# The second half block's softmax: one exponential per group of columns, its sum taken by ScalarE, its later steps moved back one slot

## The chip, the cores and the metric

The kernel runs on one core of a Trainium2 chip. The metric is the device time of one execution in microseconds (us); lower is better. The kernel before has a median of 837.12 us in three runs (836.88 to 837.44).

## The reference, cut to what matters

The reference is a linear attention with 32 memory slots, followed by a gated MLP and a mixture of eight experts. The part that this change touches is the second softmax, over the 32 memory slots of each token and head:

```python
scores = scale * np.matmul(q, k_m.transpose(0, 1, 3, 2))
scores = scores - np.max(scores, axis=-1, keepdims=True)
attn = np.exp(scores)
attn = attn / (np.sum(attn, axis=-1, keepdims=True) + 1e-09)
return np.matmul(attn, v_m).astype(np.float32)
```

Its result is the `x` of the gated MLP, `(silu(x @ w_gate) * (x @ w_val)) @ w_out`, whose hidden width of 1536 is worked off in 12 pieces of 128.

## The kernel before, in words

The 2304 tokens are cut into eight half blocks of 288 tokens (BT). Half block `i` goes through the gated MLP in 12 slots `f` (0 to 11), one for each piece of the hidden width. While half block `i` is in its slots, the softmax of half block `i+1` is prepared between them. The order of all work is written out by hand: the schedule is manual, each engine executes its instructions in the order in which the program issues them, and an engine whose next instruction waits holds back everything behind it.

`put(i, n, fn, ...)` (L688) files a step for half block `i` at time `n`; slot `f` covers the times from 2f to 2f+2. `run(i, n)` (L691) issues all steps filed up to `n`, in the order of their times. `slot0(f)` (L866) is the body of a slot of half block 0. It issues, in this order:

- the steps up to time 2f;
- in even slots the projection of the value memory (`proj_a`, L427: matmuls L346 into `pp`; `proj_h`, L435: two ScalarE copies L438; `proj_b`, L440: two VectorE subtractions L443);
- `down(0, f-2)` (L495): four matmuls L502 into `acc`;
- unpacking of arriving weights: `top(n)` (L198) is a ScalarE copy at L204, `low(n)` (L206) the VectorE instruction at L208 that needs it; in slot 9 `low(31)` and `low(32)` stand here, in slot 10 `top(33)` and `low(33)`;
- `gv(0, f)` (L469): six matmuls L473 into `pg` (PSUM bank 4), six into `pv` (bank 5), then ScalarE's Tanh of `pg` (L481);
- the steps up to 2f+1.5;
- `gate_act(0, f)` (L484): on VectorE L486, which reads `pg`, and L487, which reads `pv`;
- in slots 10 and 11 `step(34)` and `step(35)` (L857), each a `top` and its `low`;
- the steps up to 2f+1.99.

The first slot of half block 1, `slot1(1, 0)` (L895), issues `gv(1, 0)` at once. It writes the same banks 4 and 5, so its first matmul waits for the L486 of slot 11. It reads the finished softmax `X[1]`; in the order `ALL` (L466) the matmuls 1 to 3 into `pg` read group g=0 (high part, low part, high part), and 4 to 6 read g=1 (high, low, high).

The softmax of one group `g` (four heads) of one half block has these steps, on a tile `sm` of 128 partitions by 9 groups of 32 columns:

- `s2_a` (L366): VectorE's maximum over each 32 columns (L370) and its subtraction (L371);
- `s2_e` (L374): ScalarE's exponential, one instruction of 288 columns (L375);
- `s2_b` (L394): `s2_sum` (L377: VectorE's sum of each 32 columns at L379, L380 adds 1e-9, L381 takes the reciprocal) and `s2_norm` (L383: product L386 and 32x32 transpose L391, both VectorE);
- `s2_c` (L398): ScalarE's rounded copy, the high part of `X` (L401);
- `s2_d` (L403): VectorE's subtraction, the low part of `X` (L404).

A table `AT["s2"]` (L50) gives their times. Its row 0 is for half block 1, prepared in half block 0, and is read by this loop:

```python
        for g in range(2):
            for m, fn in zip((n[2], n[3], *n[4 + 3 * g:7 + 3 * g]), (s2_a, s2_e, s2_b, s2_c, s2_d)):
                if fn is s2_b and isinstance(m, tuple):
                    put(i - 1, m[0], s2_sum, i, g)
                    put(i - 1, m[1], s2_norm, i, g)
                else:
                    put(i - 1, m[g] if isinstance(m, tuple) else m, fn, i, g)
```

At 23.6 of half block 0, `s1_a` of the next batch entry is filed: two VectorE maxima of 576 columns (L270). Its exponentials `s1_e` (L275) already use ScalarE's running sum (`accum_out`), which gives an ACTIVATE and a separate ACTIVATION_READ_ACCUMULATOR.

Of the kernel before, what the change touches and what calls it, by code (L numbers as in the profile page):

```python
# [14 lines left out]
AF = mybir.ActivationFunctionType  # L15
OP = mybir.AluOpType
AX = mybir.AxisListType
# [3 lines left out]
B, H, S, D, M = 4, 8, 576, 64, 32  # L21
# [5 lines left out]
BT = S // 2  # L27
# [20 lines left out]
        2: (9, 9.92, 13.2, 13.9, 15, 17.9, 19, 19.9, 21, 21.9, 23, 23.9, 25, 25.9, 27),  # L48
    },
# [25 lines left out]
def moe_program(ctx, tc, xin, wa, wgn, nz, wb, out):  # L75
# [10 lines left out]
    V, A, P, G, Q = nc.vector, nc.scalar, nc.tensor, nc.gpsimd, nc.sync  # L86
# [251 lines left out]
    SM, X = {}, {}  # L338
# [33 lines left out]
        SM[i, g] = (sm, rd)  # L372

    def s2_e(i, g):  # L374
        A.activation(SM[i, g][0], SM[i, g][0], AF.Exp, scale=1.0 / D ** 0.5)  # L375

    def s2_sum(i, g):  # L377
        sm, rd = SM[i, g]
        V.tensor_reduce(rd[:, 1, :], sm, axis=AX.X, op=OP.add)  # L379
        V.tensor_scalar(rd[:, 1, :], rd[:, 1, :], 1e-9, None, op0=OP.add)  # L380
        V.reciprocal(rd[:, 2, :], rd[:, 1, :])  # L381

# [11 lines left out]
    def s2_b(i, g):  # L394
        s2_sum(i, g)
        s2_norm(i, g)
# [331 lines left out]
    for b in range(1, B):  # L728
        i = 2 * b - 2
# [11 lines left out]
        for j, o in enumerate(AT["proj"][b]):  # L741
            i, f = 2 * b - 1 + o // NF1, o % NF1
# [3 lines left out]
    for i in range(1, NB):  # L746
        if i > 1:
            put(i - 1, 6, load_q, i)
        n = AT["s2"].get(i - 1, AT["s2"][2])
        put(i - 1, n[0], s2_p, i)  # L750
        put(i - 1, n[1], s2_t, i)
# [33 lines left out]
    s1_cv(0, 1, 0, A)  # L785
    spin(6)
    s2_e(0, 0)
    s1_d(0, 1, 0)
    s1_dc(0, 1, 0)
# [11 lines left out]
    s1_cv(0, 1, 1, A)  # L801
    spin(14)
    s2_e(0, 1)
    s1_dc(0, 0, 1)
    s1_d(0, 1, 1)
# [748 lines left out]
```

## Time and profile before

| | |
|---|---|
| median of three runs | 837.12 us (836.88 to 837.44) |
| the profiled execution, its own time | 836.54 us |
| span of its trace | 834.7 us |
| PE busy | 820.9 us (98%) |
| DVE busy | 637.0 us (76%) |
| ACT busy | 391.8 us (47%) |
| slots 8 to 11 of half block 0 in the trace | 55.4 to 71.0 us |

PE is TensorE, DVE is VectorE, ACT is ScalarE. Times inside the trace count from the span's start. Matmuls are pipelined: each record is longer than the distance to the next one. Durations of ACT and DVE records overlap a little too, so a sum over a run of instructions is made from starts, not from durations.

### The profile page before, as it was taken

What the parts mean: (1) busy time and instruction counts of PE and PEld (TensorE: products, weight loads), DVE (VectorE), ACT (ScalarE), POOL (GpSimd) and SP (SyncE); (2) the same over time, 40 slices, a digit from 0 to 9 for tenths busy, and PEclk for the clock granted to TensorE, in tenths of its full rate; (3) what the DMA queues carried; (4) which work ended last, traced back from release to release, by engine and by line L of the source; (5) the groups of instructions that cost most, each with busy time, mean ns of one, the idle gap of its engine ahead of it and who ended that gap; (6) DMA issues with size and microseconds to landing.
All of it is one profiled execution on the core that took longest, in us unless ns stands there. A gap on an engine that the chain in (4) does not pass through costs nothing.

```text
span 834.7 us, 16643 instructions
## 1 busy us (share of the span) xinstructions
PE 820.9 (98%) x6317; PEld 730.7 (88%) x6317; DVE 637.0 (76%) x1534; ACT 391.8 (47%) x804; POOL 244.7 (29%) x345
## 2 busy tenths in 40 slices
PE   7999999999999999999999999999999999999996
PEld 5777988999899998999999988888888888888885
DVE  5887688776867677868684597898889988899761
ACT  5765565343443334333444555555455454554430
POOL 2000012424233252453122233123315233145132
PEclk9999999999999999999999999999999999999999
DMA  9993649775426373448747973555465644654421
GB/s 350 400 397 122 204 161 327 234 247 142 116 67 216 84 212 96 120 127 217 233 160 217 237 202 91 127 144 128 101 166 131 144 128 94 161 143 111 159 84 65
DMA packets 79145, 143.20 MB, mean 172 GB/s; under 512 B 16176, under 2 KB 36880, under 8 KB 79056
## 3 DMA queue, kind: packets, MB, share of 16 engines
q1 hardware_dynamic: 59696, 100.66, 38.4%
q0 software_dynamic: 19360, 41.38, 20.5%
q8 instruction: 52, 0.85, 0.4%
q14 instruction: 37, 0.30, 0.1%
HBM read 105.34 MB, written 36.68 MB: 170 GB/s over the span
## 4 chain that ended last, share of the span: by engine, by line
PE 89%; DMA 7%; DVE 2%; issue 1%; ACT 1%; SPq 0%; POOL 0%; POOLq 0%; DVEq 0%; ACTq 0%
PE acc L1190 18%; PE ph L1176 17%; PE acc L506 16%; PE pg L473 9%; PE pv L473 8%; PE acc L1005 7%; PE ph L987 7%; PE pp L346 2%; DMA out<-pv,ix 1%; DMA early<-wa 1%; DMA stw<-wa 1%; PE pT L528 1%; DMA stx<-wa 1%; DMA stg<-wa 1%; PE pkv L310 1%; DMA qt<-xin 1%
## 5 line engine op out<-in xcount | busy, mean ns | idle before, releaser
L1190 PE MATMUL acc<-ws,hs 128*128 128x512 f32 (+1 forms) x690 | 174.9, 394 | 0.0
L1176 PEld LDWEIGHTS ph<-xh,ws 128*128 128x128 f32 x1008 | 150.9, 188 | 9.7 <-ACT y L1213 0.7
L1176 PE MATMUL ph<-xh,ws 128*128 128x308 f32 x1008 | 157.4, 304 | 0.3 <-ACT y L1213 0.3
L1190 PEld LDWEIGHTS acc<-ws,hs 128*128 128x128 f32 (+1 forms) x690 | 122.7, 184 | 24.3
L506 PE MATMUL acc<-a,ro 128*128 128x288 f32 x576 | 116.4, 295 | 0.0
L1030 POOL DMA_INDIRECT out<-pv,ix x40 | 63.0, 1575 | 177.8 <-ACT pv L1022 67.5
L506 PE MATMUL acc<-a,os 128*128 128x288 f32 x432 | 106.0, 295 | 0.0
L473 PE MATMUL pg<-x,pt 128*128 128x288 f32 x576 | 101.3, 310 | 0.7 <-DVE a L486 0.2
L473 PEld LDWEIGHTS pg<-x,pt 128*128 128x128 f32 x576 | 81.0, 188 | 18.3 <-issue 6.4
L506 PEld LDWEIGHTS acc<-a,ro 128*128 128x128 f32 x576 | 92.1, 188 | 0.0
L473 PE MATMUL pv<-x,pt 128*128 128x288 f32 x576 | 91.9, 295 | 0.0
L473 PEld LDWEIGHTS pv<-x,pt 128*128 128x128 f32 x576 | 81.7, 188 | 0.0
L670 POOL DMA_INDIRECT xs<-R,gidx x48 | 48.1, 1003 | 111.5 <-DMA xs<-R,gidx 93.6
L486 DVE SCALAR_TENSOR_TENSOR ta<-ta,pg 128x288 f32<-128x288 f32 x84 | 37.6, 448 | 55.0 <-ACT ta L481 54.9
L506 PEld LDWEIGHTS acc<-a,os 128*128 128x128 f32 x432 | 74.1, 189 | 0.3 <-ACT ro L459 0.2
L481 ACT ACTIVATE ta<-pg 128x288 f32<-128x288 f32 x84 | 34.4, 410 | 82.2 <-PE pg L473 82.1
L492 ACT ACTIVATE a<-ta 128x288 fp32r<-128x288 f32 x84 | 37.3, 444 | 68.9 <-DVE ta L487 68.8
L463 POOL DMA_DIRECT2D os<-osl x72 | 40.8, 567 | 97.3 <-PE acc L506 56.0
L987 PE MATMUL ph<-xt,wm 128*128 128x384 f32 (+1 forms) x256 | 55.4, 307 | 0.0
L987 PEld LDWEIGHTS ph<-xt,wm 128*128 128x128 f32 x256 | 43.7, 189 | 2.6
L487 DVE TENSOR_TENSOR ta<-ta,pv 128x288 f32<-128x288 f32 x84 | 38.1, 454 | 8.8
L493 DVE TENSOR_TENSOR a<-ta,a 128x288 fp32r<-128x288 f32 x84 | 37.5, 447 | 5.8 <-ACT a L492 5.6
(241 smaller groups left out, 1448.1 us busy)
## 6 DMA issues: line engine op xcount, KB each, us to landing
wb<-wb SPq DMA_DIRECT2D x70, 512.0 KB, 4.4
os<-osl POOLq DMA_DIRECT2D x72, 256.0 KB, 3.4
kv<-xin SPq DMA_DIRECT2D x16, 576.0 KB, 6.5
xl<-xs SPq DMA_DIRECT2D x40, 160.0 KB, 6.7
stg<-wa SPq DMA_DIRECT2D x12, 511.8 KB, 10.2
out<-zt SPq DMA_DIRECT2D x1, 5888.0 KB, 24.7
xd<-R SPq DMA_DIRECT2D x8, 603.0 KB, 5.6
qt<-xin SPq DMA_DIRECT2D x8, 576.0 KB, 6.9
```

Source lines behind the costliest of these rows:

```text
L463: G.dma_start(r(lo), r(osl[f][:, :]))
L473: P.matmul(p, r(PT[f // 2, g][:, w, f % 2, 128 * a:128 * a + 128]), r(X[i][:, s, g, :]), start=(n == 0), stop=(n == 5))
L486: V.scalar_tensor_tensor(ta, ta, 1.0, pg, op0=OP.add, op1=OP.mult)
L487: V.tensor_mul(ta, ta, pv)
L493: V.tensor_sub(r(ah[:, 1, :]), ta, ah[:, 0, :])
L506: P.matmul(ACC[i][c], r(OS[i, f][w][:, o]), r(ah[:, s, :]), start=(f == 0 and n == 0), stop=(f == NF1 - 1 and n == 2))
L670: G.indirect_dma_start(out=xs[:, :], out_offset=bass.IndirectOffsetOnAxis(ap=RT[i][:, t, n:n + 1], axis=0), in_=R[i][:, t, :], in_offset=None)
L987: P.matmul(p, r(w[:, c]), r(x[:, k, b, :]), start=(m == 0), stop=(m == 11))
L1005: P.matmul(AC2[e, t][:h], r(a[:, o:o + h]), r(b), start=(f == 0 and m == 0), stop=(f == NF2 - 1 and m == 2))
L1030: G.indirect_dma_start(out=out, out_offset=bass.IndirectOffsetOnAxis(ap=IX[e][:h, t:t + 1], axis=0), in_=PV[e, t][:h], in_offset=None, com ...
L1176: P.matmul(out, r(w[i][:, c + 128 * k:c + 128 * k + 128]), r(x[:, m, k, a]), start=(start and n == 0), stop=(n == 5), skip_group_check=not ...
L1190: P.matmul(AC2[e, t][:h], r(a[:, n, o]), r(w[b][:, n]), start=(f == 0 and m == 0), stop=(f == NF2 - 1 and m == 2))
```

## The change

The times of the softmax steps of half block 1 become later. For group 0: the exponential from 17.1 (slot 8) to 19 (slot 9), `s2_b` from 19 to 21 (slot 10), `s2_c` from 19.9 to 21.02, `s2_d` from 21 to 21.9. For group 1: `s2_a` from 17.9 to 19.9, the exponential from 19 to 21.1, `s2_b` from 21.1 to 23 (slot 11), `s2_c` from 21.9 to 23.05, `s2_d` from 23 to 23.9. In this half block alone the exponential becomes nine instructions of 32 columns, each with ScalarE's running sum written into `rd`, and VectorE's sum (L379) goes. The other seven half blocks keep theirs.

```diff
     "s2": {
-        0: (13.9, 14, (17, 17.9), (17.1, 19), 19, 19.9, 21, 21.1, 21.9, 23),
+        0: (13.9, 14, (17, 19.9), (19, 21.1), 21, 21.02, 21.9, 23, 23.05, 23.9),
...
     def s2_e(i, g):
-        A.activation(SM[i, g][0], SM[i, g][0], AF.Exp, scale=1.0 / D ** 0.5)
+        sm, rd = SM[i, g]
+        if i == 1:
+            for a in range(BT // M):
+                A.activation(sm[:, a, :], sm[:, a, :], AF.Exp, scale=1.0 / D ** 0.5, accum_out=rd[:, 1, a:a + 1])
+        else:
+            A.activation(sm, sm, AF.Exp, scale=1.0 / D ** 0.5)
 
     def s2_sum(i, g):
         sm, rd = SM[i, g]
-        V.tensor_reduce(rd[:, 1, :], sm, axis=AX.X, op=OP.add)
+        if i != 1:
+            V.tensor_reduce(rd[:, 1, :], sm, axis=AX.X, op=OP.add)
         V.tensor_scalar(rd[:, 1, :], rd[:, 1, :], 1e-9, None, op0=OP.add)
         V.reciprocal(rd[:, 2, :], rd[:, 1, :])
```

## Rows read from the trace of the kernel before

**Rows 1.** The page: busy time of each engine.

```profile
PE 820.9 (98%) x6317; PEld 730.7 (88%) x6317; DVE 637.0 (76%) x1534; ACT 391.8 (47%) x804; POOL 244.7 (29%) x345
```

**Rows 2.** Busy time by stretch: start:end, length, PE, PEld, DVE, ACT, POOL, clock, DMA.

```profile
77.00:400.00 323.00, 322.97 (x3149) 296.91 (x3149) 235.29 (x751) 135.65 (x333) 104.10 (x214) 1.00 0.58 173
400.00:815.00 415.00, 414.75 (x2362) 369.90 (x2361) 339.20 (x652) 206.18 (x376) 129.40 (x105) 1.00 0.57 146
```

**Rows 3.** Timeline of VectorE, slots 9 to 11: start, duration, line, tiles.

```profile
60.43 1.28 DVE L208 SCALAR_TENSOR_TENSOR wa<-stg,top 128x512 int32<-128x512 int32 x2
...
62.11 0.17 DVE L380 TENSOR_SCALAR rd<-rd 128x9 f32<-128x9 f32 x1
...
63.46 0.42 DVE L486 SCALAR_TENSOR_TENSOR a<-a,pg 128x288 f32<-128x288 f32 x1
...
65.74 0.68 DVE L208 SCALAR_TENSOR_TENSOR ro<-stx,top 128x512 int32<-128x512 int32 x1
66.34 0.45 DVE L404 TENSOR_TENSOR x<-at,x 128x288 fp32r<-128x288 f32 x1
66.70 0.44 DVE L379 TENSOR_REDUCE rd<-sm 128x9 f32<-128x288 f32 x1
...
70.03 0.45 DVE L404 TENSOR_TENSOR x<-at,x 128x288 fp32r<-128x288 f32 x1
70.54 0.45 DVE L486 SCALAR_TENSOR_TENSOR a<-a,pg 128x288 f32<-128x288 f32 x1
...
71.47 0.69 DVE L208 SCALAR_TENSOR_TENSOR ro<-stx,top 128x512 int32<-128x512 int32 x1
72.07 1.41 DVE L270 TENSOR_REDUCE st<-phi 128x1 f32<-128x576 f32 x2
73.39 0.44 DVE L486 SCALAR_TENSOR_TENSOR ta<-ta,pg 128x288 f32<-128x288 f32 x1
```

**Rows 4.** Timeline of ScalarE, slots 9 to 11; in brackets the idle time before.

```profile
60.55 0.44 ACT L375 ACTIVATE sm<-sm 128x288 f32<-128x288 f32 x1
63.57 0.44 ACT L401 ACTIVATE x<-at 128x288 fp32r<-128x288 f32 x1 [2.58 <-DVE at L391]
63.92 1.07 ACT L438 ACTIVATE pt<-pp 128x512 fp32r<-128x512 f32 x2
...
70.40 0.77 ACT L204 ACTIVATE top<-stx 128x512 f16<-128x512 bf16 x1
```

**Rows 5.** The chain that ended last, in order of time, around slot 11's end.

```profile
71.05 1.06 PE pg L473 x6
72.11 0.80 PE pv L473 x6
72.91 1.94 PE acc L502 x8
```

**Rows 6.** Timeline of ScalarE: one exponential with running sum, and the next one's start.

```profile
72.85 0.78 ACT L275 ACTIVATE phi<-phi,st 128x576 f32<-128x576 f32 x1 [0.29 <-DVE st L270]
73.53 0.19 ACT L275 ACTIVATION_READ_ACCUMULATOR phi<-phi,st 128x1 f32 x1
73.63 0.76 ACT L275 ACTIVATE phi<-phi,st 128x576 f32<-128x576 f32 x1
```

**Rows 7.** Groups of ScalarE's instructions by form: busy us, mean ns of one, idle before.

```profile
L375 ACT ACTIVATE sm<-sm 128x288 f32<-128x288 f32 x16 | 6.6, 438 | 1.7 <-DVE sm L371 1.7
...
L568 ACT ACTIVATE gex<-ga 96x24 f32<-96x24 f32 x8 | 1.7, 208 | 0.0
```

**Rows 8.** Busy time by stretch again, where TensorE idles; PE second, clock eighth column.

```profile
15.00:16.00 1.00, 0.24 (x8) 0.08 (x8) 0.68 (x2) 0.97 (x2) 0.00 (x0) 1.00 1.02 414
...
827.00:828.00 1.00, 0.76 (x4) 0.26 (x2) 0.20 (x1) 0.00 (x0) 0.10 (x1) 1.00 0.35 131
...
830.00:831.00 1.00, 0.00 (x0) 0.00 (x0) 0.00 (x0) 0.00 (x0) 0.71 (x1) 1.00 0.00 0
831.00:832.00 1.00, 0.00 (x0) 0.00 (x0) 0.00 (x0) 0.00 (x0) 0.00 (x0) 0.53 0.64 148
```

## The prediction, as put on record before the changed kernel ran

> **What bounds the kernel now.** I read the page first, then busy time by stretch, the chain, and the timelines of VectorE and ScalarE around the change. The page has TensorE busy for 98% of the span [rows 1]. The stretches after the change's place say more: from 77 to 815 us TensorE is busy for 737.7 of 738 us [rows 2]. So whatever delays TensorE before 77 us is not made up later; it arrives at the end in full.
>
> The change lies in slots 9 to 11 of half block 0, about 60 to 71 us. There VectorE works with hardly a gap [rows 3] and ScalarE has one long idle stretch, 2.58 us ahead of the L401 at 63.57, where `s2_c` of group 0 waits for VectorE's transpose L391 and the projection's copies L438 queue behind it [rows 4]. Slot 11 ends with L486 at 70.54; the first matmul of half block 1 follows at 71.05, and TensorE then runs on without a break [rows 3, 5]. The time to predict is therefore when that run begins anew.
>
> **The price of one step.** No row shows a 32-column exponential with a running sum. One of 576 columns takes 0.78 us from its start to the next one's, the read of the sum included (72.85 to 73.63) [rows 6]. The slope is (438 - 208) ns over 264 columns, 0.87 ns a column [rows 7]; 544 columns fewer take off 0.47 us and leave 0.31 us a step, 2.8 us for nine, against 0.35 us until ScalarE's next start for an instruction of 288 columns (63.57 to 63.92) [rows 4]. From below: 0.208 us for an instruction of 24 columns [rows 7], less the 0.10 us by which the read began before the exponential ended, and 0.10 us for the read: 0.21 us. From above: nothing overlaps, 0.208 and 0.08 (what the 576-column one, at 0.77 us, has above 0.208 plus 552 columns by the slope) and 0.19 for the read: 0.48 us. I take 0.31, since the row of the same kind of pair is the nearest.
>
> **Slot 9.** `s2_a` of group 1 leaves its place ahead of `low(31)`; that and the missing L379 unload VectorE by 0.86 and 0.48 us, and the projection's weights are ready earlier (the last `low` before it started at 60.43) [rows 3]. It brings nothing by itself, for ScalarE now has nine steps where the exponential stood at 60.55: they end at 63.35, and the copies L438 behind them start 0.57 us earlier than 63.92 [rows 4]. What hides the steps is the 2.58 us of idle time. From there the rows repeat themselves: `low(33)` at 65.17 for 65.74 [rows 3].
>
> **Slot 10.** Behind `low(33)`, 0.60 us after its start, VectorE comes to `s2_b` of group 0 at 65.77, which before stood in slot 9. From L380 to the L401 behind the transpose took 62.11 to 63.57, so `s2_c` starts at 67.23 and the nine steps of group 1 at 67.58 [rows 3, 4]. They end at 70.38. `top(34)` queues behind them (0.8 us with the hand-over) [rows 4], and VectorE stands in front of `low(34)`, which needs it, until 71.18. This is the new wait: it holds `s2_d` of group 0 (0.60 later, 71.78), then `s2_b` of group 1 (0.36 later, 72.14), then L486 of slot 11, which comes 1.35 us after L380 (62.11 to 63.46): 73.49 [rows 3]. L486 frees bank 4, and TensorE starts half block 1 0.51 us after it, at 74.00: 2.95 us late [rows 3, 5].
>
> **Slot 11.** The second wait adds to it. Matmul 5 of the six into `pg` needs the low part of group 1, `s2_d`. It stood ahead of slot 11's L486 (70.03 and 70.54); now it stands behind `low(35)` and both L270 [rows 3]. `s2_c` starts at 72.14 + 1.46 = 73.60, `top(35)` at 73.95, `low(35)` at 74.75, L270 0.60 later at 75.35, the next VectorE instruction 1.32 later (72.07 to 73.39) at 76.67, and `s2_d` ends 0.45 later [rows 3]. With 0.04 for the hand-over matmul 5 runs at 77.16. Before, it ran at 71.05 plus four matmuls of 0.80/6 us, 71.58 [rows 5]. **The sum: 5.6 us later.**
>
> Behind matmul 5 I cost nothing: the L270 that half block 1 needs next are done by then, and the rest is queued as before. The moved steps issue no transfer, neither on SP's nor on POOL's queue, and `low(34)` and `low(35)` set no further load free. With the bounds of a step the sum moves by 18 steps: 3.8 us at 0.21 and 8.7 us at 0.48. The profiled execution took 836.54 us, the median is 837.12, 0.58 above; I put the sum on the median: **842.7 us**, with 840.9 and 845.8 at the bounds.
>
> **Rivals.** *The clock falls too.* By the sum TensorE stands from about 70 to 74.0 us, does four matmuls, and stands until 77.16. In this trace the granted clock stays at 1.00 through the emptiest early stretch (15 to 16 us, busy 0.24), but after the last matmul, which ends within 827 to 828, it is 1.00 until 831 and 0.53 in the next stretch: it falls to the lower level of 1.2 GHz [rows 8]. The new gap is longer than the first and, taken together, longer than the second, though broken by four matmuls. No row shows how soon it rises again. The work from matmul 5 to the end of L502 (71.58 to 74.85) is 3.3 us [rows 5]; at half the clock it would take up to 3.3 us more, at least nothing, and I take the middle, 1.6: 844.3 us. The Trainium skill, page "TensorE: Matmul & The Clock Gate", section "Why this matters for your kernels", warns of idle gaps between bursts of matmuls, after which the clock drops back; by that rule this rival would be the likelier, and the trace, which agrees only for its own end, leaves it open.
>
> *The steps don't overlap at all.* Then 0.48 us each, 845.8 us; against it speak the starts of rows 6, where the read begins before the exponential ends.
>
> *Not slower.* The one mechanism for it is that a step costs next to nothing: the idle 2.58 us swallows the first nine, VectorE is relieved of two L379, and each 0.01 us off a step takes 0.18 off the sum. From 0.09 us a step downward the sum is within 0.2%, 1.7 us, which is about what a measurement of this kernel can tell from no change; at 0.09 it gives 838.8 us. Against it: the read alone keeps ScalarE for 0.10 us before the next start [rows 6], and `s2_d` would still be behind L270. That the change doesn't do what it says I see no room for: the order of each engine's instructions is that of the program.
>
> **How the numbers follow.** The forecast has 0.58, the clock rival 0.27, the steps without overlap 0.08, not slower 0.05; 0.02 is left for what I don't see. The range runs from the lower bound of a step to just above its upper bound, 840.8 to 846.0 us, and holds the clock rival. Faster by over 0.2% gets 0.02, within it 0.04, slower 0.94.
>
> **What would show it.** Right: two runs of nine short exponentials with their reads on ScalarE, some 2.8 us each; L438 slightly earlier; VectorE idle ahead of `low(34)` for ScalarE's `top`; TensorE idle before its first matmul of half block 1 until about 74, and again before matmul 5 until about 77, released by VectorE's L404; the rest of the trace shifted by a constant. Wrong: the two gaps missing, L404 of group 1 ahead of L270, a run of steps far from 2.8 us, or a granted clock under 1.00 behind the gap, which would make the second case of the first.

## The result, and the profile after

The changed kernel takes 842.99 us in the median of six executions (841.37 to 844.72), the kernel before 837.21 us beside it (836.88 to 837.79): 5.78 us more, a ratio of 1.006 with an interval of 1.0047 to 1.0074. The forecast was 842.7 us. The number came out, but the sum behind it did not: one term was too large, a rival that had been given 0.27 came true on top, and the two errors cancel to the tenth.

In the changed kernel all lines from `s2_sum` on stand six higher: L473 is now L479, L486 is L492, L404 is L410, L401 is L407, L438 is L444; the exponential and its read are both at L378. The page and the stretches behind the change, against [rows 1, 2]:

```profile
PE 823.8 (98%) x6317; PEld 733.9 (87%) x6317; DVE 635.9 (76%) x1532; ACT 394.7 (47%) x838; POOL 246.1 (29%) x345
```

```profile
84.00:406.00 322.00, 321.97 (x3142) 295.92 (x3142) 233.23 (x747) 134.85 (x331) 105.80 (x214) 1.00 0.58 173
406.00:821.00 415.00, 414.75 (x2367) 370.48 (x2367) 340.69 (x655) 206.92 (x378) 129.07 (x105) 1.00 0.58 147
```

From 84 us on TensorE is as full as before; what is lost is lost ahead of that. ScalarE has 34 instructions more: 16 more exponentials and 18 reads. Its timeline in slots 9 to 11, against [rows 4]:

```profile
61.76 0.22 ACT L378 ACTIVATE sm<-sm 128x32 f32<-128x32 f32 x1
61.87 0.19 ACT L378 ACTIVATION_READ_ACCUMULATOR sm<-sm 128x1 f32 x1
61.97 0.22 ACT L378 ACTIVATE sm<-sm 128x32 f32<-128x32 f32 x1
...
63.66 1.06 ACT L444 ACTIVATE pt<-pp 128x512 fp32r<-128x512 f32 x2
...
67.53 0.44 ACT L407 ACTIVATE x<-at 128x288 fp32r<-128x288 f32 x1 [0.93 <-DVE at L397]
67.88 0.21 ACT L378 ACTIVATE sm<-sm 128x32 f32<-128x32 f32 x1
...
69.79 0.78 ACT L204 ACTIVATE top<-stx 128x512 f16<-128x512 bf16 x1
```

Nine steps take 63.66 - 61.76 = 1.90 us in slot 9 and 69.79 - 67.88 = 1.91 us in slot 10, 0.21 us a step. VectorE's timeline from slot 10 on, against [rows 3]:

```profile
67.94 0.46 DVE L493 TENSOR_TENSOR a<-a,pv 128x288 f32<-128x288 f32 x1
70.60 0.69 DVE L208 SCALAR_TENSOR_TENSOR ro<-stx,top 128x512 int32<-128x512 int32 x1 [2.20 <-ACT top L204]
71.21 0.45 DVE L410 TENSOR_TENSOR x<-at,x 128x288 fp32r<-128x288 f32 x1
71.58 0.16 DVE L386 TENSOR_SCALAR rd<-rd 128x9 f32<-128x9 f32 x1
...
72.92 0.41 DVE L492 SCALAR_TENSOR_TENSOR a<-a,pg 128x288 f32<-128x288 f32 x1
...
74.79 1.40 DVE L270 TENSOR_REDUCE st<-phi 128x1 f32<-128x576 f32 x2
76.11 0.45 DVE L410 TENSOR_TENSOR x<-at,x 128x288 fp32r<-128x288 f32 x1
```

Here are the two new waits, as the forecast placed them: VectorE stands 2.20 us ahead of `low(34)` for ScalarE's `top`, with `s2_d`, `s2_b` and L492 behind it, and `s2_d` of group 1 (76.11) comes behind both L270. TensorE's timeline shows both gaps and what follows them, against [rows 5]:

```profile
69.52 0.95 PE L479 MATMUL pv<-x,pt 128*128 128x288 f32 x6
73.39 0.98 PE L479 MATMUL pg<-x,pt 128*128 128x288 f32 x4 [2.91 <-DVE a L492]
76.61 0.85 PE L479 MATMUL pg<-x,pt 128*128 128x288 f32 x2 [2.25 <-DVE x L410]
77.26 1.64 PE L479 MATMUL pv<-x,pt 128*128 128x288 f32 x6
78.70 3.07 PE L508 MATMUL acc<-a,ro 128*128 128x288 f32 x8
81.61 0.60 PE L288 MATMUL pT<-ident,phi 128*128 128x128 f32 x4
```

After the gaps the same work is slower: six matmuls into `pv` take from 77.26 to 78.70, 1.44 us, where they took 0.80 [rows 5]. The stretches say why; the eighth column is the granted clock:

```profile
72.00:73.00 1.00, 0.00 (x0) 0.00 (x0) 0.95 (x3) 0.00 (x0) 0.00 (x0) 1.00 0.00 0
73.00:74.00 1.00, 0.61 (x4) 0.62 (x4) 0.79 (x2) 0.97 (x2) 0.00 (x0) 0.91 0.00 0
...
76.00:77.00 1.00, 0.39 (x1) 0.39 (x2) 0.56 (x2) 0.00 (x0) 0.00 (x0) 0.50 0.00 0
...
80.00:81.00 1.00, 1.00 (x4) 0.67 (x3) 0.36 (x1) 0.00 (x0) 0.00 (x0) 0.68 0.00 0
81.00:82.00 1.00, 1.00 (x8) 0.79 (x7) 0.00 (x0) 0.00 (x0) 0.00 (x0) 1.00 0.00 0
```

The clock falls to its lower level, 1.2 GHz, near the end of 73 to 74 us, when TensorE has just come out of its first gap, and is back within 80 to 81, some four us after TensorE has taken up steady work.

**One scale for all runs.** Slot 8 starts between 55.4 and 57.0 us from one execution to the next. What sets this was not tried. Both traces without the short exponentials have 55.39 us, the eight with them 56.15 to 57.03, although these steps are issued behind slot 8's start; the times of steps_alone and one_group_steps show no such cost (ratios of 0.9996 and 0.9995). So places are compared as distances from slot 8's first matmul into `pg`. "M1" and "M5" are matmuls 1 and 5 into `pg` of half block 1's first slot, "L288" is the first transpose behind that slot; the difference M5 to L288 is the same work in every kernel. M5 of the kernel before is M1 and four matmuls, as in the prediction; its own record starts at 71.68, 0.10 us later, so each "M5 later by" holds 0.10 us that is no waiting. In gap_filled, where M5 follows a wait and the clock stays up, M5 to L288 is 3.11 us too; the clock's share is counted from there. A dash stands where no wait parts M5 from M1.

| kernel | slot 8 | M1 | M5 | L288 | M1 later by | M5 later by | L288 later by | M5 to L288 |
|---|---|---|---|---|---|---|---|---|
| before | 55.39 | 71.05 | 71.58 | 74.69 | | | | 3.11 |
| changed | 56.71 | 73.39 | 76.61 | 81.61 | 1.02 | 3.71 | 5.60 | 5.00 |
| changed, again | 56.69 | 73.36 | 76.59 | 81.60 | 1.01 | 3.71 | 5.61 | 5.01 |
| gap_filled | 56.80 | 73.48 | 76.71 | 79.82 | 1.02 | 3.72 | 3.72 | 3.11 |
| low_early | 56.15 | 73.91 | - | 78.99 | 2.10 | - | 3.54 | - |
| times_alone | 55.39 | 71.13 | 74.36 | 79.55 | 0.08 | 2.78 | 4.86 | 5.19 |
| steps_alone | 57.03 | 73.10 | - | 76.73 | 0.41 | - | 0.40 | - |
| weights_first | 56.48 | 72.11 | 75.33 | 81.02 | -0.03 | 2.66 | 5.24 | 5.69 |
| both_waits_gone | 56.39 | 73.10 | - | 79.62 | 1.05 | - | 3.93 | - |
| one_group_steps | 56.79 | 72.30 | - | 75.94 | -0.15 | - | -0.15 | - |

So of the 5.60 us in the changed kernel's trace 3.71 are the waits and 1.89 (5.00 - 3.11) the clock.

### The profile page after: what moved, and what is told of

Same layout as the page of the kernel before. It is cut to its first block, busy times and chain, and to the rows that moved or that the text cites. A ratio compares the mean times of both kernels' runs of the same rounds, so it can differ in the third digit from the quotient of the medians.

```text
span 841.0 us, 16675 instructions
## 1 busy us (share of the span) xinstructions
PE 823.8 (98%) x6317; PEld 733.9 (87%) x6317; DVE 635.9 (76%) x1532; ACT 394.7 (47%) x838; POOL 246.1 (29%) x345
## 5 line engine op out<-in xcount | busy, mean ns | idle before, releaser
L479 PE MATMUL pg<-x,pt 128*128 128x288 f32 x576 | 102.2, 312 | 5.6 <-DVE a L492 2.9
L479 PEld LDWEIGHTS pg<-x,pt 128*128 128x128 f32 x576 | 81.3, 189 | 22.9 <-issue 6.4
L479 PE MATMUL pv<-x,pt 128*128 128x288 f32 x576 | 92.6, 296 | 0.0
L479 PEld LDWEIGHTS pv<-x,pt 128*128 128x128 f32 x576 | 82.4, 189 | 0.0
L492 DVE SCALAR_TENSOR_TENSOR ta<-ta,pg 128x288 f32<-128x288 f32 x84 | 37.6, 448 | 57.5 <-ACT ta L487 56.2
```

The costliest lines, as they stand in the source:

```text
L479: P.matmul(p, r(PT[f // 2, g][:, w, f % 2, 128 * a:128 * a + 128]), r(X[i][:, s, g, :]), start=(n == 0), stop=(n == 5))
L492: V.scalar_tensor_tensor(ta, ta, 1.0, pg, op0=OP.add, op1=OP.mult)
```

## The experiments

The first four ran on one chip beside each other (the kernel before: 837.61 us there), the last four on another (838.11 us). Each diff is against the changed kernel. Executions scatter more there, so ratios have wide intervals, and the distances of the table carry the verdicts.

**The gaps filled with matmuls that nobody reads** (gap_filled).

```diff
+    def spin6(n):
+        p = bank(6, [128, 128], "spin")
+        for _ in range(n):
+            P.matmul(p, ones, ones, start=True, stop=True)
...
             for n, (w, s, g) in enumerate(FEW if i == f == 0 else ALL):
+                if (i, f, a, n) == (1, 0, 0, 4):
+                    spin6(32)
...
         gv(0, f)
+        if f == NF1 - 1:
+            spin6(40)
```

> The changed kernel, with matmuls that nobody reads put into TensorE's two new gaps: 40 of 128 columns behind slot 11's pv, 32 between matmul 4 and matmul 5 of half block 1's first slot, into a PSUM bank that is free there. Every wait on the softmax stays. Theory (two waits of 3.8 us in sum, and a clock that falls in the gap they leave, 1.7 us more): the granted clock stays at 1.00, matmul 5 still runs at about 5.0 us behind its place in the kernel before, the first L288 follows it after 3.3 us and not 5.0, and the time is about 841.3 us, 1.7 below the changed kernel. Rival (the clock's dip costs nothing, the waits are the whole loss): 843.0 us, unchanged.

Measured: 841.63 us, ratio 1.0042 (1.002 to 1.0064), where the changed kernel itself has 1.006 and, run again, 1.0055. TensorE's timeline and two of the stretches that stood at 0.91 and 0.50 (its line numbers are five to seven higher again):

```profile
70.41 2.41 PE L271 MATMUL spin<-ones 128*128 128x128 bf16 x40
73.48 0.80 PE L486 MATMUL pg<-x,pt 128*128 128x288 f32 x4 [0.67 <-DVE a L499]
74.12 1.96 PE L271 MATMUL spin<-ones 128*128 128x128 bf16 x32
76.71 0.54 PE L486 MATMUL pg<-x,pt 128*128 128x288 f32 x2 [0.63 <-DVE x L415]
79.82 0.60 PE L293 MATMUL pT<-ident,phi 128*128 128x128 f32 x4
```

```profile
73.00:74.00 1.00, 0.52 (x4) 0.52 (x4) 0.88 (x3) 0.88 (x2) 0.00 (x0) 1.00 0.00 0
76.00:77.00 1.00, 0.37 (x4) 0.29 (x3) 0.66 (x2) 0.00 (x0) 0.00 (x0) 1.00 0.00 0
```

M1 and M5 are as late as in the changed kernel (1.02 and 3.72 us), the clock stays at 1.00, and M5 to L288 is back at 3.11 us. (The expected 5.0 us count from the span's start: 76.71 - 71.58 = 5.13.) The theory holds: waits and clock are two separate losses. The trace parts them; the times agree, but their intervals overlap.

**The low part of group 1 earlier** (low_early).

```diff
-        0: (13.9, 14, (17, 19.9), (19, 21.1), 21, 21.02, 21.9, 23, 23.05, 23.9),
+        0: (13.9, 14, (17, 19.9), (19, 21.1), 21, 21.02, 21.9, 23, 23.05, 23.06),
```

> The changed kernel with the low part of group 1 (s2_d) at 23.06 in place of 23.9: ahead of slot 11's reading of pg, low(35) and the two maxima L270. Theory (the second wait is s2_d behind these): the wait ahead of matmul 5 goes; slot 11's L492 and with it the first matmul come 0.9 us later, since VectorE waits for s2_c and then does s2_d first; matmul 5 runs 1.7 us earlier than in the changed kernel; if the clock falls all the same, the time is about 841.3 us; if a single gap of about 3.8 us leaves the clock alone, 839.6 us. Rival (matmul 5 waits for something else): unchanged, 843.0 us.

Measured: 840.79 us, ratio 1.0031 (1.0013 to 1.005). The wait ahead of matmul 5 is gone, M1 moves from 1.02 to 2.10 us late, and L288 from 5.60 to 3.54:

```profile
73.91 1.78 PE L479 MATMUL pg<-x,pt 128*128 128x288 f32 x6 [4.00 <-DVE a L492]
```

One gap of 4.00 us is left, and the clock falls in it (0.88 in 73 to 74 us, 0.50 in the next, 0.91 in 77 to 78). M1 to L288 takes 5.08 us against 3.64, so the clock costs 1.44 here. Matmul 5 starts at 75.01, 1.04 us earlier than in the changed kernel and not 1.7, since M1 comes 1.08 later and the four matmuls take 1.10 us at the lower clock, where they took 0.63. The second wait was `s2_d` behind slot 11's L492, `low(35)` and both L270, as forecast.

**The new times alone** (times_alone).

```diff
-        sm, rd = SM[i, g]
-        if i == 1:
-            for a in range(BT // M):
-                A.activation(sm[:, a, :], sm[:, a, :], AF.Exp, scale=1.0 / D ** 0.5, accum_out=rd[:, 1, a:a + 1])
-        else:
-            A.activation(sm, sm, AF.Exp, scale=1.0 / D ** 0.5)
+        A.activation(SM[i, g][0], SM[i, g][0], AF.Exp, scale=1.0 / D ** 0.5)
...
-        if i != 1:
-            V.tensor_reduce(rd[:, 1, :], sm, axis=AX.X, op=OP.add)
+        V.tensor_reduce(rd[:, 1, :], sm, axis=AX.X, op=OP.add)
```

> The kernel before with the new times alone: one exponential of 288 columns a group, and VectorE's sum as before. Theory (the loss is mostly the steps' 1.9 us in front of top(34) and the order of slot 11; the steps themselves make some 1.5 us a group on ScalarE, of which the second group's stands on the path): low(34) hardly waits, the first matmul of half block 1 comes about 0.1 us later than before, matmul 5 about 2.7 us later, behind L270; 839.9 us, or 841.5 if the clock falls there. Rival (the times are harmless, the steps cost all): 837.2 us. Rival (the times cost all): 843.0 us.

Measured: 842.78 us, ratio 1.0062 (1.0039 to 1.0085). The trace (with the line numbers of before):

```profile
71.13 0.80 PE L473 MATMUL pg<-x,pt 128*128 128x288 f32 x4 [1.98 <-DVE a L486]
74.36 0.85 PE L473 MATMUL pg<-x,pt 128*128 128x288 f32 x2 [2.42 <-DVE x L404]
```

```profile
71.00:72.00 1.00, 0.80 (x4) 0.57 (x4) 0.61 (x3) 0.89 (x2) 0.00 (x0) 0.98 0.00 0
72.00:73.00 1.00, 0.00 (x0) 0.00 (x0) 1.00 (x2) 0.00 (x0) 0.00 (x0) 0.50 0.00 0
```

M1 is 0.08 us late and M5 2.78, against 0.1 and 2.7 expected; the clock falls and takes 5.19 - 3.11 = 2.08 us. So the times alone make 4.86 of the changed kernel's 5.60 us. The time lies above the 841.5 us expected with the clock's fall, and its interval, 840.9 to 844.7 us, holds the second rival's 843.0 too: the times can't tell the two kernels apart, the trace does.

**The steps alone** (steps_alone).

```diff
-        0: (13.9, 14, (17, 19.9), (19, 21.1), 21, 21.02, 21.9, 23, 23.05, 23.9),
+        0: (13.9, 14, (17, 17.9), (17.1, 19), 19, 19.9, 21, 21.1, 21.9, 23),
```

> The kernel before with the nine steps and ScalarE's sums alone, at the old times. Theory: ScalarE gets 1.55 us more in slot 8 ahead of three top copies, and in slot 9 ahead of the projection's copies, where it idled; VectorE is relieved of 0.96 us; matmul 5 stays within 0.5 us of its place; 837.6 us, not to be told from the kernel before. Rival (the steps cost all): 843.0 us.

Measured: 837.85 us, ratio 0.9996 (0.9975 to 1.0017); M1 and L288 are 0.41 and 0.40 us late, and the clock stays up. At the old times the steps hold up the weights instead: the projection's second half waits 1.44 us for VectorE's L208, where it waited 0.30 us in the kernel before.

```profile
64.56 0.67 PE L346 MATMUL pp<-wa,km 64*32 64x256 f32 x16 [1.44 <-DVE wa L208]
...
73.10 1.06 PE L479 MATMUL pg<-x,pt 128*128 128x288 f32 x6 [0.20 <-DVE a L492]
```

**The changed kernel again** (after_again), without an edit.

> The changed kernel as it is, beside the others. Every theory: 1.006 times the kernel before; matmul 5 of half block 1's first slot 19.9 us behind slot 8's first matmul into pg, against 16.2 in the kernel before; granted clock 0.50 behind the gap.

Measured: 844.11 us, ratio 1.0055 (1.0034 to 1.0075), with the same distances as in the first trace within 0.01 us. In its eight executions the mean granted clock is 0.990 to 0.994.

**The weights first** (weights_first).

```diff
             top(LATE)
             low(LATE)
+            step(todo.pop(0))
```

> The changed kernel with top(34) and low(34) issued in slot 10 right behind top(33) and low(33), ahead of slot 10's softmax steps. Theory (VectorE's 2.2 us of waiting ahead of low(34) is what makes the first matmul late): this wait goes, but s2_b of group 1 then waits for the nine steps themselves, which come 0.6 us later behind a later s2_b of group 0; the first matmul and matmul 5 both run some 1.2 us earlier than in the changed kernel; the clock falls as before; 1.2 us less. Rival (the wait at low(34) is only a place where VectorE would wait anyway): no change in either matmul.

Measured: 842.91 us, ratio 1.0059 (1.0033 to 1.0085). VectorE's 2.20 us ahead of `low(34)` are gone, and a wait of 1.15 us for the steps themselves stands in their place:

```profile
70.29 0.17 DVE L386 TENSOR_SCALAR rd<-rd 128x9 f32<-128x9 f32 x1 [1.15 <-ACT sm L378]
```

M1 and M5 come 1.05 us earlier than in the changed kernel (1.2 expected). But L288 gains only 0.36, since the clock, which falls within TensorE's second gap, takes 5.69 - 3.11 = 2.58 us here. The first wait is confirmed; the time does not show it.

**Both waits gone** (both_waits_gone): the edits of low_early and weights_first together.

> The changed kernel with both: top(34) and low(34) first, and s2_d of group 1 at 23.06. Theory: the first matmul of half block 1 some 0.8 us later than in the kernel before, no wait ahead of matmul 5; one gap of about 3 us. If the clock stays at 1.00, 0.8 us above the kernel before; if one gap of that length is enough for it to fall, 2.5 us above. Rival (something else in the new times is late): 1.5 us or more behind in matmul 5.

Measured: 839.59 us, ratio 1.0016 (0.9998 to 1.0035). M1 is 1.05 us late (0.8 expected) and nothing waits behind it. In the profiled execution the clock fell in the one gap of 2.95 us that is left, and L288 is 3.93 us late, 2.88 of them by the clock. It had fallen once before, far ahead of the change (0.50 from 18 to 21 us), which is ahead of slot 8 and so in no distance, but in the execution's mean clock of 0.993. The 12 executions have means between 0.989 and 0.997, and their median is 1.5 us above the kernel before, between the 0.8 expected without a fall and the 2.5 with one: how many of them fell behind the change isn't shown.

```profile
73.10 1.78 PE L479 MATMUL pg<-x,pt 128*128 128x288 f32 x6 [2.95 <-DVE a L492]
```

```profile
18.00:19.00 1.00, 1.00 (x14) 0.74 (x22) 0.81 (x4) 0.90 (x4) 0.00 (x0) 0.50 1.11 442
...
72.00:73.00 1.00, 0.00 (x0) 0.00 (x0) 0.82 (x2) 0.77 (x2) 0.00 (x0) 0.72 0.00 0
```

**Steps for group 1 alone, at the old times** (one_group_steps).

```diff
-        0: (13.9, 14, (17, 19.9), (19, 21.1), 21, 21.02, 21.9, 23, 23.05, 23.9),
+        0: (13.9, 14, (17, 17.9), (17.1, 19), 19, 19.9, 21, 21.1, 21.9, 23),
...
-        if i == 1:
+        if (i, g) == (1, 1):
...
-        if i != 1:
+        if (i, g) != (1, 1):
```

> The kernel before at its old times, with nine steps and ScalarE's sum for group 1 alone, whose exponential stands in slot 9 where ScalarE idles 2.6 us. Theory: the steps fit into the idle time, VectorE loses one sum of 0.48 us, and slot 11's end, which waits for the Tanh of TensorE's own product, does not move: within 0.1 us of the kernel before in matmul 5, not to be told from it in time. Rival (VectorE's work bounds these slots, so each sum taken off it is gained): 0.5 us less.

Measured: 838.02 us, ratio 0.9995 (0.9974 to 1.0017); M1 0.15 us earlier than in the kernel before. VectorE is done sooner and then waits for the Tanh:

```profile
71.79 0.46 DVE L492 SCALAR_TENSOR_TENSOR a<-a,pg 128x288 f32<-128x288 f32 x1 [0.29 <-ACT a L487]
```

This is the best of the versions, and not to be told from the kernel before. None of the versions beats the kernel before by more than a measurement can show.

## Why the prediction was right, and where it was not

**Place and kind of the loss: right.** TensorE has nothing behind 77 us to make up a delay, and the shift arrives at the end: the span grows by 6.3 us, of which 5.6 lie between slot 8 and L288; slot 8 started 1.3 us later in this execution, and what lies behind L288 is 0.6 us shorter (841.0 - 81.61 against 834.7 - 74.69). Both waits stand where the steps on slots 10 and 11 put them, with the releasers named there. weights_first takes the first away and moves M1 and M5 by 1.05 us (1.2 expected); low_early takes the second away.

**The price of one step: too high.** The failing step is the subtraction for 544 columns, which left 0.31 us of the 0.78 in [rows 6]; measured are 0.21. In the changed trace the read starts 0.12 us behind its exponential of 32 columns, in [rows 6] 0.68 us behind one of 576: a difference of 0.56 us, where the prediction took off 0.47. The missing 0.09 can be a steeper slope under a running sum (1.03 ns a column for 0.87) or a fixed part of the long exponential. Rows speak for the fixed part: L275 reads its bias from a column of `st`, the short exponentials have no such operand. In the kernel before, two copies of one shape out of PSUM, one with a column of factors (`ml`) and one without, last 681 and 594 ns, 0.087 us apart:

```profile
L1022 ACT ACTIVATE pv<-acc,ml 128x512 f32<-128x512 f32 x28 | 18.0, 681 | 2.4 <-PE acc L1005 1.4 <-DMA out<-pv,ix 0.9
...
L297 ACT ACTIVATE en<-pT 128x512 f32<-128x512 f32 x8 | 4.8, 594 | 0.5 <-PE pT L288 0.5
```

And the running sum doesn't lengthen the short records: 0.21 to 0.22 us for 32 columns with it, 0.208 for 24 without [rows 7]. The prediction saw this part, the 0.08 in its upper bound, and left it in the 0.31. No run changes the operand alone, so the reason is argued from rows and not shown; the price of 0.21 is measured.

At the lower bound, also 0.21, the prediction's sum was 3.8 us; M5 is 3.71 us late. M1, forecast 2.95 us late at 0.31, is 1.02 late.

**The clock: a rival that should have been part of the sum.** It was priced at 1.6 us and costs 1.89. gap_filled shows it apart from the waits. The prediction took the stretch of 15 to 16 us [rows 8], which left the clock alone, as evidence against it; but TensorE still worked for a quarter of that stretch, and the new gaps have nothing in them but four matmuls. Nor is that early part safe from a fall: in both_waits_gone the clock went down within 17 to 18 us. The rule of the Trainium skill, page "TensorE: Matmul & The Clock Gate", section "Why this matters for your kernels", that idle gaps between bursts bring the clock down, would have given the better chance; the trace of the changed kernel agrees with it (0.50 from 74 to 80 us).

**What cancelled.** 5.6 forecast was 18 steps too dear by 0.10 us, 1.8 us, and the clock's 1.9 us left out. The forecast's number is right by this accident; as a sum of the waits alone it was 1.9 us too high.

**The share of the parts.** The prediction said that the steps take no time in slot 9 and hold the path in slot 10. times_alone adds that the later times would cost nearly as much without them: 2.78 of the 3.71 us are there without a short exponential, nearly all of them `s2_d` of group 1 behind slot 11's L486, `low(35)` and both L270, and the steps add 0.93.

**Not slower: ruled out** by the interval, 1.0047 at its lower end. Even a step of 0.21 us, a third cheaper than taken, left 3.71 us of waiting, and times_alone shows why cheap steps would not have saved it: the order of slot 11 is a loss by itself. The prediction gave a step of 0.09 us a loss of 1.6 us; times_alone, whose exponential keeps ScalarE for less than nine such steps would, still has M5 2.78 us late, some of it VectorE's sums, and the clock's fall on top.

## What to carry to other kernels

A step that is moved later in a written-out order must be held against the first instruction that needs it and against everything that the new place puts ahead of it on its own engine: here the work on VectorE that `s2_d` was put behind cost the path some 2.7 us, the eighteen short exponentials 0.9. Where an edit opens a gap on TensorE, count the clock as a part of the loss from the start: two gaps of two to three us with four matmuls between them cost another 1.9 us, half of what the waits themselves cost. A price taken over from another instruction should be held against its operands first: the row that the 0.31 us came from has a bias column that the new instructions lack.

## What the runs showed of the hardware that had not been expected

An exponential of 32 columns with its read into memory costs ScalarE 0.21 us in a run of them, though each of the two records alone lasts about 0.2 us: the read starts 0.12 us behind the exponential, the next exponential 0.09 to 0.10 us behind the read.

The granted clock fell also where no single gap was long: in times_alone it was 0.98 in 71 to 72 us and 0.50 in the next, so it went down at the end of 71 to 72 us, when only a gap of 1.98 us and four matmuls lay behind and the second gap was just beginning. A fall cost 2.08 us there, 1.89 in the changed kernel, 1.44 in low_early, 2.58 in weights_first and 2.88 in both_waits_gone; it differs with where the fall lies against the work. By which rule the gaps of these kernels sum up was not tried; filling them with unread matmuls kept the clock at 1.00.
